# Filler matmuls at the start: the first ones on zeros, and a lower bar for the gaps that get them

## The chip, the cores and the metric

The kernel runs on one core of a Trainium2 chip. The metric is the device time of one execution in microseconds; of several runs the median is taken. Three runs of the kernel before took 624.91, 627.36 and 629.05 us, so the median is 627.36 us. The engines are named as in the profile: PE (TensorE matmuls, with PEld for its weight loads), DVE (VectorE), ACT (ScalarE), POOL (GpSimd) and SP (SyncE, which here only issues DMAs).

## What is computed

Block-causal attention over 8 batches, 8 heads, 576 positions and 64 columns per head, then a gated feed-forward network with a convolution over three positions:

```python
scores = scale * np.matmul(q, k.transpose(0, 1, 3, 2))      # 576 x 576 per head
scores = np.where(block_i >= block_j, scores, -1e9)          # blocks of 64
attn = exp(scores - max) / (sum + 1e-09)
x = (attn @ v)                                               # heads side by side: 576 x 512
h = np.maximum(x @ w_in, 0.0)                                # 512 -> 1024
conv_out = conv_w[0] * h[s - 1] + conv_w[1] * h[s] + conv_w[2] * h[s + 1]
out = (h * sigmoid(conv_out)) @ w_out                        # 1024 -> 512
```

## The kernel before, in words

Two heads are handled together as a pair; a batch has four pairs. For batch 0 each pair is done in two parts, first the first 256 positions (`stage_sa`, score products in line 1336, reductions to the row maximum in line 1354, exponentials in line 1362), then the rest (`stage_sb`, lines 1275 and 1291, with `last_s`, line 1123, for the last 64 positions). From batch 1 on a pair is done in one piece (`stage_s`, products in line 1111, maxima in line 1210, exponentials in line 1213). The probabilities are turned (line 1410, by matmuls with an identity) and multiplied with v (lines 1454 and 1494). The feed-forward network (`ffn`) multiplies with the two halves of w_in in line 1547 and with those of w_out in line 1640; the weights are decoded and split at the start by DVE, ACT and POOL (lines 885 to 963).

The order is written by a planner. Every operation is given to `Plan.op` with an engine, an estimated duration and a target; a long table of numbers replaces the targets. `Plan.order` then plays a clock of its own for five engines: `free[PE]` is the planned time at which PE is free, and it starts at zero (SP's at 0.75). It takes the operation that can start first and gives PSUM banks to tiles as it goes. The order in which operations come out is the order in which each engine's instructions are issued; semaphores hold the real order.

**Fills.** When the planner sees PE idle for longer than `LEAST` (0.4 us of planned time) and a PSUM bank is free, it puts matmuls there that compute nothing which is used: each multiplies the 128x128 identity (`rident`) with itself into 512 columns of the free bank (`work`, line 1777). Their number is the gap, less `SPARE` (0.09), divided by 0.234 us (twice that while the planner believes PE's clock to be low). In the kernel before there are 80 of them, in 17 places, the last of them 158 us into the span. A fill that has the tile `rident` as its operand cannot start before DVE has written that tile (line 645), which itself waits for POOL's `ident`. In `work` the operand would be the zeros in `blank` for any fill emitted before that write; since the write is emitted ahead of all fills, none uses it. `blank` is the first thing DVE writes (line 666).

The first products of the program are those of line 1336 for pair 0. They need q (loaded by SP's queue, scaled by POOL in line 1018) and k, whose DMA for this pair alone is issued by ACT's queue (line 701). Between pair 0 and pair 1 stands the small transpose of the convolution weights (line 1003).

Of the kernel before, what the change touches and what calls it, by code (L numbers as in the profile page):

```python
# [220 lines left out]
class Plan:  # L221
# [56 lines left out]
    def order(self, targets, fill, clock):  # L278
# [37 lines left out]
            for d in o.deps:  # L316
                d.outs.append(o)
        rtime, wtime, early = ([0.0] * len(self.ops) for _ in range(3))
        free = [0.0, 0.0, 0.0, 0.0, 0.75]
        port, begun, tail, moved = [0.0, 0.0, 0.0], -1.0, 0.2, 0.0  # L320
        done = []
        for _ in self.ops:
# [26 lines left out]
            if e == PE and t - free[PE] > least and t > begin:  # L349
                spot = [(max(free[PE], begun, freed[z]), z) for z in range(n) if tenant[z] is None]  # L350
                if spot:
# [3 lines left out]
                    if k > 0:  # L355
                        x = Op()
# [63 lines left out]
def kernel(  # L420
# [51 lines left out]
    JW = (JW0, JW1, JW2, JW3, JW4, JW5, JW6, JW7, JW8, JW9, JWA, JWB, JWC, JWD, JWE, JWF)  # L472
    JD = (JD0, JD1, JD2, JD3, JD4, JD5, JD6, JD7, JL8, JL9, JLA, JLB, JLC, JLD, JLE, JLF)
    EBLK = (2,3)
    LEAST, SPARE = 0.4, 0.09
    CLOCK = (3.413, 0.46, 0.33, 1.0, 0.098)
    GROUPS = {"A": ((0, 1),), "B": ((2,), (3,)), None: ((0, 1, 2), (3,))}
    NORMS = {"A": (), "B": (), None: ()}
# [159 lines left out]
    make_identity(nc, ident)  # L638
    rident = cp.tile([P, P], F32R, tag="rident", name="rident")

    rounded_one = []

    def rounded_identity():
        rounded_one.append(rident)
        nc.vector.tensor_scalar(out=rident, in0=ident, scalar1=1.0, scalar2=None, op0=ALU.mult)

    def constant(x, value):
# [3 lines left out]
        return go  # L651

    made = [pl.op(DVE, 0.2, rounded_identity, -80.0)]
    maskt = cp.tile([P, 64], F32R, tag="maskt", name="maskt")
    made.append(pl.op(ACT, 2.8, constant(maskt, MASKED), -80.0))
# [9 lines left out]
    blank = cp.tile([P, P], F32R, tag="blank", name="blank")  # L665
# [1102 lines left out]
    fills = []  # L1768

    def work(slot, k):  # L1770
        fills.append(k)

        def go():
            x = rident if rounded_one else blank
            b = psum[:, 512 * slot:512 * slot + 512]
            for _ in range(k):
                nc.tensor.matmul(b.rearrange("p (c n) -> p c n", n=P), x,
                                 x.unsqueeze(1).broadcast_to([P, 4, P]), start=True, stop=True)

        return go  # L1780

    ctx.enter_context(tc.manual_schedule(engines=None))
    for o in pl.order([int(x) for x in TARGETS.split()], (work, psum, 0.234, LEAST, SPARE), CLOCK):
        o.fn()
# [86 lines left out]
```

## Time and profile before

| | |
|---|---|
| profiled execution, device time | 626.53 us |
| its span, first to last instruction | 624.6 us |
| median of the three timed runs | 627.36 us (624.91 to 629.05) |
| mean granted TensorE clock | 0.995 |
| PE busy | 593.6 us, 95% |
| DVE busy | 536.5 us, 86% |
| ACT busy | 480.2 us, 77% |
| POOL busy | 388.8 us, 62% |

About 1.9 us of the profiled execution lie outside the span. Busy shares are means over stages with different limits. Where a row names who released an engine from its wait ("<-"), the name is the one whose signal came last. The ends of matmuls are modelled, so the ends of rows on PE are less exact than their starts.

### The profile page before, as it was taken

The numbers are of one execution on the slowest core, as the hardware profiler recorded it, in microseconds if no ns is written. First come the engines' busy times: TensorE is split into PE (matmuls) and PEld (weight loads), VectorE is DVE, ScalarE is ACT, GpSimd is POOL, SyncE is SP. The second block draws the span as 40 slices with busy tenths as digits, with TensorE's granted clock in tenths as the row PEclk, the third lists the DMA queues.
The fourth block names the chain that finished last, engine by engine and source line by source line (L and its number), as shares of the span: only waits on it lengthen the run. The fifth ranks groups of instructions, "written<-read, shape, count | busy, mean of one in ns | idle before, by whom it ended". The sixth has DMA issues, their size and how long they took to land.

```text
span 624.6 us, 15535 instructions
## 1 busy us (share of the span) xinstructions
PE 593.6 (95%) x5823; PEld 378.1 (61%) x5823; DVE 536.5 (86%) x1124; ACT 480.2 (77%) x1231; POOL 388.8 (62%) x498
## 2 busy tenths in 40 slices
PE   7888899977999999999999999999999999999997
PEld 4556554456765567655775577555765667566754
DVE  6999989999889988999999996999989957982741
ACT  5999998787688769997998687888787757963730
POOL 4876545584496656986687645765897615742630
PEclk9998989999999999999999999999999999999999
DMA  8783402799928996689966699179955970595002
GB/s 297 236 314 116 132 22 81 172 219 193 260 48 182 233 232 127 132 214 214 214 159 154 138 213 266 48 131 217 218 105 103 230 145 18 108 150 130 1 1 84
DMA packets 205503, 97.76 MB, mean 157 GB/s; under 512 B 185308, under 2 KB 187636, under 8 KB 205428
## 3 DMA queue, kind: packets, MB, share of 16 engines
q1 hardware_dynamic: 203844, 94.16, 68.1%
q10 hardware_dynamic: 1584, 2.62, 1.3%
q8 instruction: 45, 0.74, 0.5%
q14 instruction: 30, 0.25, 0.1%
HBM read 41.44 MB, written 9.44 MB: 81 GB/s over the span
## 4 chain that ended last, share of the span: by engine, by line
PE 37%; DVE 36%; ACT 10%; POOL 9%; issue 4%; DMA 3%; SPq 0%; ACTq 0%; DVEq 0%; POOLq 0%
PE banks L1640 14%; PE banks L1547 12%; DVE su L1210 7%; PE banks L1494 4%; PE banks L1111 4%; POOL t L1589 3%; DVE ptbl L1066 3%; DVE t L1576 2%; DVE ptbm L1066 2%; DVE t L1595 2%; POOL shared L1606 2%; DVE shared L900 1%; ACT t L1592 1%; DVE shared L895 1%; ACT p3f L1213 1%
## 5 line engine op out<-in xcount | busy, mean ns | idle before, releaser
L1640 PE MATMUL banks<-woh,shared 128*128 128x512 f16 (+1 forms) x592 | 184.0, 374 | 1.3 <-ACT p2f L1213 0.9
L1547 PE MATMUL banks<-x,wih 128*128 128x288 f16 (+2 forms) x1024 | 158.3, 288 | 5.1 <-ACT p4f L1213 1.6
L1640 PEld LDWEIGHTS <-shared 128*128 128x128 f16 x888 | 82.7, 98 | 101.3 <-issue 14.0
L1547 PEld LDWEIGHTS <-wih 128*128 128x128 f16 x1024 | 98.4, 98 | 40.5 <-issue 11.9
L1210 DVE TENSOR_REDUCE su<-banks 128x1 f32<-128x384 f32 (+8 forms) x252 | 110.2, 477 | 6.1 <-PE banks L1111 4.2
L1640 PE MATMUL banks<-wol,shared 128*128 128x512 f16 (+1 forms) x296 | 110.5, 373 | 0.0
L1589 POOL TENSOR_TENSOR t<-t,shared 128x575 f32<-128x575 f32 x51 | 73.4, 1440 | 49.4 <-DVE t L1576 44.9
L1547 PE MATMUL banks<-x,wil 128*128 128x288 f16 (+2 forms) x512 | 86.6, 287 | 0.0
L1111 PE MATMUL banks<-k,q 64*64 64x192 f32 (+9 forms) x1120 | 82.6, 417 | 3.3 <-ACT p1f L1213 1.3
L1606 POOL TENSOR_TENSOR shared<-t,shared 128x576 f16<-128x576 f32 (+2 forms) x57 | 71.3, 1253 | 16.8 <-ACT shared L1599 8.0
L1494 PEld LDWEIGHTS <-vb 128*64 128x64 f16 x1848 | 61.8, 111 | 12.6 <-issue 12.5
L1576 DVE SCALAR_TENSOR_TENSOR t<-banks,cwb,t 128x575 f32<-128x575 f32 (+2 forms) x72 | 53.4, 743 | 14.9 <-ACT t L1572 8.1
L1111 PEld LDWEIGHTS banks<-k,q 64*64 64x64 f32 x1120 | 43.0, 133 | 33.0 <-issue 14.1
L1592 ACT ACTIVATE t<-t 128x576 f32<-128x576 f32 (+2 forms) x72 | 45.1, 627 | 21.1 <-POOL t L1589 14.3
L1595 DVE SCALAR_TENSOR_TENSOR t<-t,banks 128x576 f32<-128x576 f32 (+2 forms) x72 | 48.9, 680 | 12.2 <-ACT t L1592 11.4
L1547 PEld LDWEIGHTS <-wil 128*128 128x128 f16 x512 | 49.5, 98 | 13.9 <-issue 0.6
L1572 ACT ACTIVATE t<-banks,cwb 128x576 f32<-128x576 f32 (+2 forms) x72 | 49.2, 685 | 2.0 <-POOL shared L1606 0.5
L1566 ACT ACTIVATE banks<-banks 128x576 f32<-128x576 f32 (+2 forms) x54 | 30.9, 577 | 18.6 <-PE banks L1547 16.7
L1585 ACT ACTIVATE shared<-banks,cwb 128x575 f32<-128x575 f32 x51 | 37.7, 738 | 8.6 <-DVE banks L1569 7.2
L1213 ACT ACTIVATE p3f<-banks,su 128x512 f32<-128x512 f32 (+1 forms) x56 | 36.8, 660 | 5.6 <-DVE su L1210 3.0
L1650 ACT ACTIVATE stage<-banks,osc 128x512 f32<-128x512 f32 (+1 forms) x27 | 18.0, 675 | 25.3 <-PE banks L1640 22.5
L1213 ACT ACTIVATE p1f<-banks,su 128x192 f32<-128x192 f32 (+1 forms) x56 | 24.9, 446 | 15.4 <-DVE su L1210 12.6
(204 smaller groups left out, 1190.4 us busy)
## 6 DMA issues: line engine op xcount, KB each, us to landing
k<-in_k_dram SPq DMA_DIRECT2D x28, 368.0 KB, 3.8
vn<-in_v_dram SPq DMA_DIRECT2D x32, 320.0 KB, 3.8
q<-in_q_dram SPq DMA_DIRECT2D x28, 320.0 KB, 3.6
out_dram<-stage SPq DMA_DIRECT2D x26, 256.0 KB, 3.0
shared<-in_moe_w_in_dram SPq DMA_DIRECT2D x8, 512.0 KB, 4.6
shared<-in_moe_w_out_dram SPq DMA_DIRECT2D x8, 512.0 KB, 4.7
out_dram<-stage ACTq DMA_DIRECT2D x9, 256.0 KB, 4.2
k<-in_k_dram SPq DMA_DIRECT2D x4, 240.0 KB, 5.6
```

The lines of the kernel that those rows point to most:

```text
L1111: nc.tensor.matmul(out[64 * y:64 * y + 64], t["q"].ap[64 * r:64 * r + 64, q0:q0 + 64], t["k"].ap[64 * r:64 * r + 64, k0:k0 + c1 - c0], sta ...
L1210: nc.vector.tensor_reduce(out=st.ap[:, k:k + 1], in_=home[hh].ap[:, x], op=ALU.max, axis=AX.X, negate=True)
L1213: nc.scalar.activation(out=y.ap[:, 0:n], in_=home[hh].ap[:, x], func=AF.Exp, bias=st.ap[:, k:k + 1], accum_out=st.ap[:, 9 + k:10 + k])
L1494: nc.tensor.matmul(y, vb.ap[:, w, c, j, :], x, start=first, stop=(z == 1 and c == jobs[-1][0]), skip_group_check=True)
L1547: nc.tensor.matmul(h(a, z), wt[:, c, fs], xs[c][xi].ap[:, x0 + a:x0 + z], start=(n + c - c0 == 0), stop=(n + c - c0 == 3 * NCC - 1))
L1572: nc.scalar.activation(out=t.ap[:, 0:no], in_=h(own, own + no), func=AF.Copy, scale=cwb.ap[:, NFC + f:NFC + f + 1])
L1576: nc.vector.scalar_tensor_tensor(out=t.ap[:, i0:no], in0=h(own + i0 - 1, own + no - 1), scalar=cwb.ap[:, f:f + 1], in1=t.ap[:, i0:no], op0 ...
L1589: nc.gpsimd.tensor_tensor(out=t.ap[:, 0:i1], in0=t.ap[:, 0:i1], in1=u.ap[:, 0:i1], op=ALU.add)
L1592: nc.scalar.activation(out=t.ap[:, 0:no], in_=t.ap[:, 0:no], func=AF.Tanh)
L1595: nc.vector.scalar_tensor_tensor(out=t.ap[:, 0:no], in0=t.ap[:, 0:no], scalar=1.0, in1=h(own, own + no), op0=ALU.add, op1=ALU.mult)
L1606: eng.tensor_tensor(out=g[1][:, f, carry:carry + no], in0=t.ap[:, 0:no], in1=g[0][:, f, carry:carry + no], op=ALU.subtract)
L1640: nc.tensor.matmul(fb.ap[:, 0:cut], g[a][:, f, cs], w[:, f, ds], start=(f == 0 and n == 0), stop=(f == NFC - 1 and n == 2))
```

## The change

Four edits. `free[PE]` starts at 1.1 instead of 0.0, so that the planner puts nothing on PE before 1.1 us of its own clock. `LEAST` falls from 0.4 to 0.25 and `SPARE` from 0.09 to 0.0, so that shorter planned gaps get fills and each gap may get one more. The first group of fills multiplies the zeros in `blank`, every other group `rident` as before (it is decided when the plan is made, by the count of groups so far). The list that was to tell whether `rident` had been written goes away, and with it two lines, so that every line behind it has a number lower by two.

```diff
-        free = [0.0, 0.0, 0.0, 0.0, 0.75]
+        free = [1.1, 0.0, 0.0, 0.0, 0.75]
...
-    LEAST, SPARE = 0.4, 0.09
+    LEAST, SPARE = 0.25, 0.0
...
-    rounded_one = []
 
     def rounded_identity():
-        rounded_one.append(rident)
         nc.vector.tensor_scalar(out=rident, in0=ident, scalar1=1.0, scalar2=None, op0=ALU.mult)
...
     def work(slot, k):
         fills.append(k)
+        x = rident if len(fills) > 1 else blank
 
         def go():
-            x = rident if rounded_one else blank
             b = psum[:, 512 * slot:512 * slot + 512]
```

On DVE, ACT, POOL and SP the instructions and their order are the same as before, and every tile keeps its PSUM bank. On PE only fills differ: 89 in 21 places instead of 80 in 17.

PE at the start of the program, before (`rident` is the identity, `cg` the convolution weights, `maskt` the mask that is added):

```order
L1777 MATMUL banks<-rident 128x512 x7
L1336 MATMUL banks<-k,q 128x128 x2
L1340 MATMUL banks<-maskt,rident 64x64 x2
L1336 MATMUL banks<-k,q 128x256 x2
L1340 MATMUL banks<-maskt,rident 64x64 x2
L1003 MATMUL banks<-ident,cg 128x24
L1777 MATMUL banks<-rident 128x512 x4
L1336 MATMUL banks<-k,q 128x128 x2
```

The same place with the change (`blank` is the tile of zeros):

```order
L1775 MATMUL banks<-blank 128x512 x5
L1334 MATMUL banks<-k,q 128x128 x2
L1338 MATMUL banks<-maskt,rident 64x64 x2
L1334 MATMUL banks<-k,q 128x256 x2
L1338 MATMUL banks<-maskt,rident 64x64 x2
L1775 MATMUL banks<-rident 128x512
L1001 MATMUL banks<-ident,cg 128x24
L1775 MATMUL banks<-rident 128x512 x5
L1334 MATMUL banks<-k,q 128x128 x2
```

Seven fills on the identity became five on zeros, and two more fills stand between the products of pair 0 and those of pair 1.

PE at the last turns of batch 0's third and fourth tile rows, ahead of the first products of a pair of batch 1, before (`p3r` are probabilities, `ptbh` turned ones):

```order
L1410 MATMUL banks<-rident,p4r_98 128x128 x4
L1410 MATMUL banks<-rident,p3r_94 128x128 x4
L1410 MATMUL banks<-rident,p3r_96 128x128 x4
L1777 MATMUL banks<-rident 128x512
L1111 MATMUL banks<-k,q 64x64 x2
L1111 MATMUL banks<-k,q 64x512 x2
```

The same place with the change:

```order
L1408 MATMUL banks<-rident,p4r_98 128x128 x4
L1408 MATMUL banks<-rident,p3r_94 128x128 x4
L1408 MATMUL banks<-rident,p3r_96 128x128 x4
L1775 MATMUL banks<-rident 128x512 x2
L1109 MATMUL banks<-k,q 64x64 x2
L1109 MATMUL banks<-k,q 64x512 x2
```

One fill became two. The other places that gain a fill: one ahead of pair 2's products of line 1336, one in a group of nine, one ahead of line 1454 (at 27.6 us before), one each in the groups at 34.9, 44.7, 70.1 and 143.4 us, and one ahead of the products of line 1111 at 100.7 us.

## Rows read from the trace of the kernel before

**Rows 1.** The page: busy time by engine; the chain that ended last, by engine.

```profile
PE 593.6 (95%) x5823; PEld 378.1 (61%) x5823; DVE 536.5 (86%) x1124; ACT 480.2 (77%) x1231; POOL 388.8 (62%) x498
...
PE 37%; DVE 36%; ACT 10%; POOL 9%; issue 4%; DMA 3%; SPq 0%; ACTq 0%; DVEq 0%; POOLq 0%
```

**Rows 2.** Chain that ended last, start: start us, us, what.

```profile
1.44 1.00 DVE rident L645
...
2.48 3.35 PE banks L1777 x7
5.83 0.73 PE banks L1336 x4
...
7.72 0.94 DVE st L1354 x3
```

**Rows 3.** Timeline of PE, 2 to 11 us: start, us, line, tiles [idle before].

```profile
2.48 3.35 PE L1777 MATMUL banks<-rident 128*128 128x512 f32 x7 [2.48 <-DVE rident L645]
5.76 0.80 PE L1336 MATMUL banks<-k,q 64*128 64x128 f32 x4
...
7.06 0.62 PE L1340 MATMUL banks<-maskt,rident 64*64 64x64 f32 x2
7.61 0.29 PE L1003 MATMUL banks<-ident,cg 24*128 24x24 f32 x1
7.84 1.20 PE L1777 MATMUL banks<-rident 128*128 128x512 f32 x4
8.96 0.49 PE L1336 MATMUL banks<-k,q 64*128 64x128 f32 x4
...
9.64 0.39 PE L1340 MATMUL banks<-maskt,rident 64*64 64x64 f32 x2
10.56 0.49 PE L1336 MATMUL banks<-k,q 64*128 64x128 f32 x4 [0.54 <-ACT q L1021]
```

**Rows 4.** Timeline of DVE and of ACT's DMA queue, same stretch.

```profile
0.83 0.17 DVE L666 MEMSET blank<- 128x128 f32 x1 [0.83 <-PEq L1854]
...
1.44 0.38 ACTq L701 DMA_DIRECT2D k<-in_k_dram  x1
...
7.71 0.95 DVE L1354 TENSOR_REDUCE st<-banks 128x1 f32<-128x256 f32 x3 [3.29 <-PE banks L1340]
...
10.59 2.23 DVE L1354 TENSOR_REDUCE st<-banks 128x1 f32<-128x128 f32 x8
```

**Rows 5.** DMA issues of the first 12 us: KB each, us to landing.

```profile
k<-in_k_dram ACTq DMA_DIRECT2D x1, 128.0 KB, 4.0
```

**Rows 6.** Stretches: busy us of each engine, granted clock (PEclk), DMA.

```profile
55.64:59.05 3.41, 1.49 (x14) 1.17 (x13) 3.41 (x8) 3.22 (x11) 3.33 (x4) 1.00 0.49 154
59.05:62.46 3.41, 3.41 (x20) 2.62 (x19) 3.41 (x8) 2.64 (x9) 2.95 (x4) 0.50 0.68 167
...
79.53:82.94 3.41, 3.41 (x21) 1.70 (x21) 2.78 (x4) 3.04 (x9) 3.33 (x5) 0.50 0.00 0
```

**Rows 7.** Timeline of PE around later places that gain a fill.

```profile
27.59 2.28 PE L1454 MATMUL banks<-ptbh,vn 128*64 128x320 f32 x20 [0.54 <-ACT ptbh L679]
...
34.87 1.67 PE L1777 MATMUL banks<-rident 128*128 128x512 f32 x6 [1.23 <-ACT p1f L1362]
36.68 0.88 PE L1410 MATMUL banks<-rident,p3r 128*128 128x128 f32 x8
...
71.78 1.13 PE L1275 MATMUL banks<-k,q 64*128 64x512 f32 x4 [0.29 <-DVE st L1134]
```

**Rows 8.** Chain that ended last, 45 to 105 us.

```profile
46.26 1.99 DVE wil L963 x3
...
79.48 1.21 PE banks L1410 x8
80.68 0.55 PE banks L1777
81.24 1.93 PE banks L1111 x8
...
83.26 0.83 DVE su L1210 x2
...
104.86 5.99 PE banks L1640 x27
```

## The prediction

> **What bounds the kernel now.** I read the page first. PE is busy for 593.6 of 624.6 us, but the chain that ended last is shared: 37% of it on PE and 36% on DVE [rows 1]. So the kernel has stages with different limits, and the change must be read where it acts: in the first 160 us, and there above all in the first 12, since fills stand nowhere later.
>
> Second, the chain of waits at the start. It runs from DVE's writing of the identity (1.44 us) through the seven fills (2.48 to 5.83) to the first score products of line 1336 and from 7.72 on through DVE, beginning with the maxima of line 1354 [rows 2]. Behind that it stays mostly on DVE up to the turns of 79.48 [rows 8]. The reader is to see that PE is late only once in the opening, at DVE's idle 3.29 us ahead of 7.71 [rows 4].
>
> Third, the timeline of PE there [rows 3]. The chain makes it look as if the fills held the products back. The DMA view says otherwise: k for pair 0 is issued by ACT's queue from 1.44 for 0.38 us [rows 4] and lands 4.0 us after that [rows 5], 1.44 + 0.38 + 4.0 = 5.82 within the rounding of the view. The products start at 5.76 [rows 3]. So the first product waits for k, and the seventh fill happened to end just then.
>
> Fourth, PE's clock. In the opening the duration of equal work tells it: seven fills take 3.35 us, 0.48 each, at 2.48 [rows 3]; six take 1.67, 0.28 each, at 34.87 [rows 7]. The products of pair 0 take from 5.76 to 7.06 + 0.62 = 7.68, 1.92 us; the same work for pair 1 from 8.96 to 9.64 + 0.39 = 10.03, 1.07 us [rows 3]. So PE ran at its lower level (1.2 GHz) up to about 7.7 and at 2.4 GHz soon after, having worked without a pause from 2.48. Twice more the granted clock is 0.50 for 3.41 us: at 59.05, after a stretch in which PE was busy for 1.49 of 3.41 us, and at 79.53 [rows 6].
>
> **The change part by part.**
>
> *Fills on zeros.* They need only `blank`, written at 0.83 to 1.00 [rows 4], not the identity. So PE can begin at about 1.05 instead of 2.48. Five fills at 0.48 end at about 3.5. The wait for the identity leaves the chain, but k still lands at 5.8, so the products start at 5.76 as now: the direct gain is 0. The mask products behind them now wait for the identity themselves; it is there by 2.44 [rows 2].
>
> *The clock at 5.76.* PE will have worked 2.4 us by 3.5 and then stand idle for 2.2 us. If the clock is up when k lands, pair 0's products take 1.07 us instead of 1.92: 0.85 us less, and since DVE waits for exactly them, it begins line 1354 at 6.86 instead of 7.71. If it is not, the gain is 0. The trace before shows neither case, so these are the bounds. I take 0.85: the fills' 2.4 us fall 1.4 us earlier, and all of pair 0's work lay in the slow stretch that the clock's rise ended at about 7.7, so any rise before 5.76 takes the whole of it.
>
> *Two more fills between pair 0 and pair 1* (one ahead of line 1003, one in the group of four). They delay pair 1's products by at most 2 x 0.28 = 0.56 us. Pair 1's products would end at 10.03 - 0.85 + 0.56 = 9.74; DVE, also 0.85 earlier, asks for them at 10.59 - 0.85 = 9.74 [rows 3, 4]. That is just covered: cost 0. If the first term fails, the cover is the 0.56 us between 10.03 and 10.59, again just enough at the higher clock. The fill ahead of pair 2 lies in the 0.54 us for which PE waits for ACT's q at 10.56 [rows 3]: 0.
>
> *Later fills.* The new one ahead of line 1454 lies in a wait of 0.54 us, and the sixth of 70.1 in front of one of 0.29 [rows 7]: 0 each. The seventh at 34.87 would end where the turns of 36.68 start anyway, 34.87 + 1.67 + 0.28 = 36.82 at most with the drain of the last counted in [rows 7], and DVE carries the chain there: 0. The fourth at 44.7 and the tenth at 17.9 stand where the chain is on DVE, as at 46.26 [rows 8]: 0; if that cover were gone, 0.28 each. The one ahead of line 1111 at 100.7 waits for DVE's earlier signal, and PE's work behind it waits again before it takes the chain at 104.86 [rows 8]: 0. The one at 143.4 likewise, 0 to 0.28.
>
> *The second fill at 80.7* is the exception. The chain goes through PE there: turns, one fill of 0.55, products, then DVE's maxima at 83.26 [rows 8]. The clock is at its lower level from 79.53 to 82.94 [rows 6], so one more fill costs about 0.48; at the higher level 0.28. I take +0.48.
>
> **Does the start reach the end?** 0.85 us earlier at 7.7 is worth something only if DVE stays the limit. DVE's share of the chain is as large as PE's [rows 1], and no DMA stands in the opening's rows of it [rows 2]. I let it pass whole; that it is lost on the way belongs to the second case below.
>
> **The sum**, against the profiled execution: 626.53 - 0.85 + 0.48 = 626.16 us. The median of the three runs, 627.36, lies 0.83 above that execution; the same step brings the forecast to **627.0 us**. In the last 65 us and in most of the middle no instruction changes.
>
> **The rivals.**
>
> A, the forecast: the clock is up by 5.76. Chance 0.40.
>
> B, nothing is gained at the start: the five fills on zeros do not raise the clock in time, or in most timed runs of the kernel before it was already up when k landed. For it: five fills are fewer than seven, and a pause of 2.2 us follows. Then only the fill at 80.7 counts: 627.36 + 0.48 = 627.8. Chance 0.29. The Trainium skill, page "TensorE: Matmul & The Clock Gate", Part 1 ("What's actually happening"), says that the moment of the rise is not tied to a kernel's start, so that the same kernel shows different numbers of slow matmuls from run to run. By that rule the gain is 0.85 in some executions and 0 in others, and the sum would be about 627.4, half way; one execution before cannot show it.
>
> C, slower: the pause keeps the clock down for longer. Before, PE's work was unbroken from 2.48 until the rise at about 7.7; now a pause of 2.2 us lies in it. If the clock is not up by 7.7, the next stretch is slow as well: a fill (0.48), line 1003 and five fills (2.4) bring PE from 7.7 to about 10.8, and pair 1's products, partly slow, end near 12.1 instead of 10.03, 2.05 late less the 0.56 that DVE has to spare, +1.5. With the fill at 80.7: 627.36 + 1.5 + 0.48 = 629.3. It decides if the products behind 7.7 are still slow. Against it: PE works without a pause from 5.76 on in that case too. Chance 0.19.
>
> D, the low clock at 79.53 goes away, because an earlier start or the sixth fill at 70 moves the quiet stretch ahead of it. Turns of eight take 0.88 at the higher clock [rows 7] and 1.21 there [rows 8]; with the fill and about half of the 1.93 of line 1111 some 1.5 us of the chain go, and the fill costs 0.28. On top of A: 627.36 - 0.85 - 1.5 + 0.28 = 625.3. Chance 0.12.
>
> That the change would not do what it says is small: the order shows the five fills on zeros first.
>
> **How the numbers follow.** The likeliest case gives 627.0. The cases lie between 625.3 and 629.3, and a median of runs that spread over 624.9 to 629.05 moves by about 1 us, so 8 in 10 needs **624.5 to 629.9**. A difference of 1% is 6.3 us, about what a measurement of this kernel can tell from no change; no row holds so much, all the fills added amount to 9 x 0.48 = 4.3 us even if none were covered. Faster by over 1%: 0.03; within 1%: 0.94; slower by over 1%: 0.03. These rests are for an effect of the shifted order that I do not see.
>
> **What would show it.** In the changed profile five fills on `blank` begin at about 1.05 and the first products still at 5.76. Right for A: pair 0's products take about 1.07 us and DVE's first maxima come at 6.9. B: they take 1.92 and DVE starts at 7.7. C: pair 1's products take well over 1.07 us and DVE waits ahead of its second maxima. D: no granted clock of 0.50 near 79. The chain should hold two fills of together about 1 us near 80. I am wrong if the products start well before 5.7, if one of the covered fills appears in the chain, or if the middle of the span, where nothing was changed, differs by more than the start does.

## The result, and the profile after

The changed kernel takes **629.94 us** (median of 5 runs, 629.31 to 631.30) where the kernel before took 626.54 (median of 5, 624.59 to 629.05): 1.0061 times as long, 95% interval 1.0042 to 1.0080. The forecast was 627.0 with a range up to 629.9. The median lies only 0.04 us beyond the range, and a second set of runs (f1 below) has 629.45, inside it; what is plainly wrong is the direction. The forecast step was -0.4 us (from 627.36, the median of three runs that was then known), the measured one is +3.4 here and +2.7 in f1. That is the side of rival C (629.3), which had a chance of 0.19. By the bound of 1% the result is still "within 1%".

The profiled execution after took 629.94 us, its span is 627.9 (before 626.53 and 624.6 [rows 1]). The page gives the busy time by engine, and the share of each engine in the chain of waits:

```profile
PE 596.1 (95%) x5832; PEld 380.8 (61%) x5832; DVE 536.5 (85%) x1124; ACT 480.6 (77%) x1231; POOL 388.5 (62%) x498
...
PE 43%; DVE 31%; POOL 9%; ACT 9%; DMA 5%; issue 3%; SPq 0%; ACTq 0%; DVEq 0%; POOLq 0%
```

PE's share of the chain rose from 37 to 43% at DVE's expense. The chain of waits from the start (start us, us, what) answers to [rows 2]:

```profile
1.45 4.67 DMA k<-in_k_dram
...
6.26 0.80 PE banks L1334 x4
...
8.17 0.72 PE banks L1775
8.89 0.23 PE banks L1001
9.12 2.43 PE banks L1775 x5
11.55 0.54 PE banks L1334 x4
```

The load of k stands at its head now, as the prediction said, and the identity is gone from it. But six fills (line 1775) have come into it behind pair 0's products; before, DVE had the chain from 7.72 on. The timeline of PE (start, us, line, tiles, idle before) answers to [rows 3]:

```profile
1.05 2.50 PE L1775 MATMUL banks<-blank 128*128 128x512 f32 x5 [1.05 <-DVE blank L664]
6.26 0.80 PE L1334 MATMUL banks<-k,q 64*128 64x128 f32 x4 [2.70 <-DMA k<-in_k_dram]
...
7.53 0.65 PE L1338 MATMUL banks<-maskt,rident 64*64 64x64 f32 x2
8.10 0.79 PE L1775 MATMUL banks<-rident 128*128 128x512 f32 x1
8.83 0.30 PE L1001 MATMUL banks<-ident,cg 24*128 24x24 f32 x1
9.05 2.50 PE L1775 MATMUL banks<-rident 128*128 128x512 f32 x5
11.49 0.61 PE L1334 MATMUL banks<-k,q 64*128 64x128 f32 x4
...
12.29 0.38 PE L1338 MATMUL banks<-maskt,rident 64*64 64x64 f32 x2
```

Read the fives: the five fills at 9.05 take 2.50 us, as long as the five at 1.05, which is 0.48 to 0.5 each and so the lower level (1.2 GHz). Before, the four at 7.84 took 1.20 [rows 3]. Pair 0's products and masks take 6.26 to 8.18, 1.92 us, just as before. Pair 1's last product ends at 12.29 + 0.38 = 12.67; before it was 10.03. In this trace the first recorded change of the granted clock, to full, is at 11.77 us; in that of before it is at 7.85. Up to here the one idle time of PE that is new is the pause of 2.70 us ahead of 6.26.

DVE's timeline shows who pays; it answers to [rows 4]:

```profile
8.18 0.95 DVE L1352 TENSOR_REDUCE st<-banks 128x1 f32<-128x256 f32 x3 [3.71 <-PE banks L1338]
...
12.71 1.15 DVE L1352 TENSOR_REDUCE st<-banks 128x1 f32<-128x128 f32 x4 [1.57 <-PE banks L1338]
```

The second maxima (those of pair 1) come at 12.71 instead of 10.59, 2.12 us late, behind a wait for PE that did not exist before. It stays: at DVE's first write of the tile `wil`, which started at 45.0 before, the changed kernel is at 47.4, 2.4 late (groups of one tile, first the kernel before and then the changed one; behind the durations stand the first start and the last start):

```profile
L963 DVE SCALAR_TENSOR_TENSOR wil<-shared,fac,wih x8: 731/738/884, 45.0 to 58.9; 128x512 f16<-128x512 f32 x8
L961 DVE SCALAR_TENSOR_TENSOR wil<-shared,fac,wih x8: 732/740/905, 47.4 to 61.4; 128x512 f16<-128x512 f32 x8
```

The DMA view answers to [rows 5]: k took 4.7 us to land where it took 4.0, so the products begin at 6.26 instead of 5.76.

```profile
k<-in_k_dram ACTq DMA_DIRECT2D x1, 128.0 KB, 4.7
```

That half microsecond is the execution's and not the change's: a second profile of the same kernel (f1 below) has the products at 5.78 and the second maxima at 12.97.

The stretches (us, busy us of PE, PEld, DVE, ACT and POOL, granted clock, DMA) answer to [rows 6]:

```profile
59.05:62.46 3.41, 2.16 (x21) 1.98 (x22) 3.41 (x7) 3.41 (x12) 3.24 (x4) 1.00 0.47 154
79.53:82.94 3.41, 3.00 (x26) 2.01 (x28) 3.29 (x8) 3.41 (x12) 3.03 (x4) 1.00 0.00 0
428.20:431.61 3.41, 1.36 (x15) 0.59 (x14) 3.38 (x11) 1.09 (x5) 1.38 (x2) 1.00 1.19 188
431.61:435.02 3.41, 3.07 (x50) 3.07 (x51) 0.87 (x3) 3.41 (x14) 0.31 (x1) 0.50 1.05 237
```

The two low stretches of before, at 59.05 and 79.53, are not in this execution; one at 431.61 is. Around 79.5 the chain answers to [rows 8]: PE is no longer in it, so the second fill there costs nothing.

```profile
80.89 0.39 DVE su L1208
81.28 0.70 DVE shared L898
...
84.13 0.82 DVE su L1208 x2
```

At 431 the chain goes through the output's write, from which the buffer `stage` comes free, and then through products at the low clock (1.2 GHz):

```profile
424.85 6.26 DMA out_dram<-stage
...
431.21 0.70 ACT stage L1648
431.95 3.75 PE banks L1492 x65
```

In the trace of before the same write took 5.24 us, and the products behind it start at 430.38 at the full clock (a line of its chain and one of its PE timeline):

```profile
424.30 5.24 DMA out_dram<-stage
...
430.38 1.07 PE L1494 MATMUL banks<-ptbx,vb 128*64 128x256 f16 x20 [1.34 <-ACT stage L1650]
```

DVE's lateness against that trace, instruction by instruction, is 2.33 us at 12.9, 2.56 at 59.7, 0.85 at 86 (where before had its own low stretch), 0.52 at 426.5 and 3.27 at 438 (moments of the trace of before). So two accounts were open: the start's 2.1 to 2.5 us last to the end and the profile of before only hides them by its own two low stretches; or they are regained in the middle, and the loss is the new stretch at 431.

### The profile page after: what moved, and what is told of

Same layout as the page of the kernel before. It is cut to its first block, busy times and chain, and to the rows that moved or that the text cites. A ratio compares the mean times of both kernels' runs of the same rounds, so it can differ in the third digit from the quotient of the medians.

```text
span 627.9 us, 15554 instructions
## 1 busy us (share of the span) xinstructions
PE 596.1 (95%) x5832; PEld 380.8 (61%) x5832; DVE 536.5 (85%) x1124; ACT 480.6 (77%) x1231; POOL 388.5 (62%) x498
## 4 chain that ended last, share of the span: by engine, by line
PE 43%; DVE 31%; POOL 9%; ACT 9%; DMA 5%; issue 3%; SPq 0%; ACTq 0%; DVEq 0%; POOLq 0%
PE banks L1638 17%; PE banks L1545 14%; DVE su L1208 6%; PE banks L1492 6%; PE banks L1109 5%; POOL t L1587 3%; DVE ptbl L1064 3%; POOL shared L1604 2%; DVE t L1574 2%; DVE ptbm L1064 2%; DVE t L1593 2%; DMA k<-in_k_dram 2%; ACT t L1590 1%; DVE vb L832 1%; DVE shared L898 1%
## 5 line engine op out<-in xcount | busy, mean ns | idle before, releaser
L1492 PEld LDWEIGHTS <-vb 128*64 128x64 f16 x1848 | 63.3, 113 | 13.6 <-issue 12.9
```

The source lines that it names most:

```text
L1492: nc.tensor.matmul(y, vb.ap[:, w, c, j, :], x, start=first, stop=(z == 1 and c == jobs[-1][0]), skip_group_check=True)
```

## The experiments

The kernels were run in three series (e, f, g). Each kernel has 12 runs against 35 runs of the kernel before in the same series. Ratios are to those, with 95% intervals. The medians of before in the three series were 627.18, 626.79 and 627.26. Fills compute nothing that is used, so every one of these kernels does the whole computation. Line numbers shift by one or two between them. The last two columns come from the one execution of each that was profiled: the moment at which the granted clock rose to full, and the start of DVE's second maxima.

| run | what it is | median us | ratio | clock rises, us | second maxima, us |
|---|---|---|---|---|---|
| f1 | the change, again | 629.45 | 1.0040 [1.0017, 1.0064] | 12.93 | 12.97 |
| e1 | the change, old bar of 0.4 | 629.41 | 1.0026 [1.0000, 1.0051] | 9.88 | 10.93 |
| e2 | before, new bar of 0.25 | 628.05 | 1.0017 [0.9998, 1.0036] | 6.36 | 10.07 |
| e3 | the change, 11 zeros for 5 | 626.80 | 0.9998 [0.9978, 1.0017] | 6.88 | 10.57 |
| e4 | the change, no fills between pairs 0 and 1 | 629.66 | 1.0031 [1.0014, 1.0048] | 15.79 | 11.02 |
| f2 | 11 zeros and the old bar | 627.15 | 0.9998 [0.9979, 1.0018] | 5.56 | 9.90 |
| f3 | the change, third `stage` buffer | 628.25 | 1.0012 [0.9990, 1.0035] | 13.75 | 13.44 |
| f4 | before, 5 fills for 7 | 626.90 | 1.0008 [0.9988, 1.0029] | 14.56 | 12.31 |
| g1 | before, third `stage` buffer | 626.06 | 0.9982 [0.9958, 1.0006] | 6.35 | 10.46 |
| g2 | f2 and the third `stage` buffer | 625.10 | 0.9971 [0.9948, 0.9995] | 4.92 | 9.85 |
| g3 | f2, 16 fills for 4 ahead of pair 1 | 628.14 | 1.0013 [0.9990, 1.0036] | 4.40 | 12.12 |
| g4 | before, 2 fills for 7 | 629.72 | 1.0041 [1.0015, 1.0066] | 14.40 | 12.12 |

The record also gives the mean granted clock of each execution. It does not see the opening, where the column reads 1.00 throughout; it falls by 0.5 x 3.41 / 625 = 0.0027 for one low stretch in the middle. So it tells roughly how many of those stretches an execution had. Of the 105 executions of the kernel before, 21 have 0.999 or more (mean 625.36 us), 60 have 0.996 to 0.998 (627.13) and 24 less (628.20).

**Which half of the change is it?** e1 keeps the start on zeros and puts the bar back; e2 does the reverse.

```
e1, against the change:
-    LEAST, SPARE = 0.25, 0.0
+    LEAST, SPARE = 0.4, 0.09
e2, against before:
-    LEAST, SPARE = 0.4, 0.09
+    LEAST, SPARE = 0.25, 0.0
```

> Only the start is changed: five fills on zeros from 1.05 us, planned from 1.1; LEAST and SPARE stay 0.4 and 0.09, so four fills stand between pair 0 and pair 1 and one fill ahead of 81 us. Theory P (the pause after the zeros keeps the clock low until about 11.8 us, and fills at the low clock then hold back pair 1's products): the clock rises near 11 to 12 us, DVE's second maxima start at about 12.0 (10.59 in the kernel before, 12.7 with the whole change; one fill and a half microsecond less than there), and the time is 1.5 to 3 us over the kernel before. Theory B (the lowered bar with its added fills costs the time): the second maxima start within 0.5 us of 10.6 to 11.1 and the time is that of the kernel before within 1 us.

> Only the bar is changed: LEAST 0.25 and SPARE 0.0; the first group is seven fills on the identity from 2.48 us as before. Theory P: the clock rises before 8.5 us as in the kernel before, DVE's second maxima start at 10.6 to 11.2, and the time is within 1 us of the kernel before. Theory B: DVE's second maxima start near 12 to 12.7 and the time is 2 to 4 us over the kernel before.

The start alone takes 0.26% more, the bar alone 0.17%; the first interval touches 1 and the second covers it. The runs point to the start but do not separate the two. The execution of e1 that was profiled was its fastest, 625.09 against a median of 629.41, and its clock rose at 9.88 already, so its page says little of the median.

**Is it the pause?** e3 leaves all of the change in and makes the first group 11 zeros, so that PE works right up to the arrival of k. If the pause is the cause, the loss goes; if it is that zeros do not count as work, or the eleven fills that the bar adds behind the first group (84 on the identity for 73 in e1), it stays.

```
-            for _ in range(k):
+            for _ in range(k if x is rident else 11):
```

> The whole change, but the first group is eleven fills on zeros instead of five, so that PE works without a pause from 1.05 us to about 5.9, when k lands. Theory P: the clock is up before the first products or at the latest where it was before (7.85), pair 0's products take 1.07 to 1.92 us, DVE's second maxima start at 9.8 to 10.7, and the time is 0 to 1 us under the kernel before. Theory Z (matmuls on zeros do not raise the clock, whatever their number): the clock rises at about 11.8 as with the whole change, the second maxima start at 12.7, and the time is 2 to 4 us over the kernel before.

The loss is gone, 0.9998. Its PE timeline:

```profile
1.05 5.06 PE L1775 MATMUL banks<-blank 128*128 128x512 f32 x11 [1.05 <-DVE blank L664]
6.24 0.78 PE L1334 MATMUL banks<-k,q 64*128 64x128 f32 x4
...
8.12 1.42 PE L1775 MATMUL banks<-rident 128*128 128x512 f32 x5
9.47 0.49 PE L1334 MATMUL banks<-k,q 64*128 64x128 f32 x4
```

The products start at 6.24, as late as in the profile after, yet the five fills at 8.12 take 1.42 us and not 2.50: the granted clock rose at 6.88. Pair 1 begins at 9.47, two microseconds before the changed kernel's. The bar's eleven fills are all still there, so they cost nothing that can be measured once the clock is up, and the clock rises behind zeros too. What e3 does not separate is the pause from the amount: it closes the pause by more than doubling the fills.

**Is it the six fills, which the prediction's rival C put in the way?** e4 takes only them out.

```
+        n = 0 if len(fills) in (2, 3) else k
...
-            for _ in range(k):
+            for _ in range(n):
```

> The whole change without the six fills between pair 0's and pair 1's products (one ahead of the small transpose, five behind it). If it is the fills at the low clock in front of pair 1's products that make DVE late, those products start at about 8.4 instead of 11.5, end at about 10.3 even at the low clock, and DVE's second maxima start at about 11.0 instead of 12.7: the time is 1 to 2 us under the whole change. If it is the low clock itself, whatever stands in the queue, the second maxima stay within 0.5 us of 12.7.

The time stays where it was (1.0031). PE's and DVE's timelines show why:

```profile
8.29 0.80 PE L1334 MATMUL banks<-k,q 64*128 64x128 f32 x4
...
10.99 0.80 PE L1334 MATMUL banks<-k,q 64*128 64x128 f32 x4
...
12.29 0.62 PE L1338 MATMUL banks<-maskt,rident 64*64 64x64 f32 x2
```

```profile
11.02 1.12 DVE L1352 TENSOR_REDUCE st<-banks 128x1 f32<-128x128 f32 x4
12.95 0.95 DVE L1352 TENSOR_REDUCE st<-banks 128x1 f32<-128x128 f32 x3 [0.81 <-PE banks L1338]
```

Four products take 0.80 us (0.49 at the full clock [rows 3]) at 8.29 and still at 10.99; here the clock rose only at 15.79. The second maxima are earlier, at 11.02, but the next wait for the slow products, and by 47.0 the first write of `wil` is as late as in the change. With the six fills the clock rose at 11.77 to 13.75 in three profiles (the change, f1, f3), without them at 15.79 in this one. So it may be that the fills both lengthen the bill of the low clock and help to end it, which one profile does not show; taking them out moved the bill and did not lower it by the 1 to 2 us that I expected.

**Does the change repeat, and is the new bar needed for the repair?** f1 is the change unaltered, f2 is e3 with the old bar.

```
f2, against the change:
-    LEAST, SPARE = 0.25, 0.0
+    LEAST, SPARE = 0.4, 0.09
...
-            for _ in range(k):
+            for _ in range(k if x is rident else 11):
```

> The whole change once more, unaltered. The earlier look showed one execution in which DVE was 2.3 us late at the start, 0.5 late at 421 us and 3.3 late at the end, with a stretch of low clock at 431.6. If the late end is that of the start alone (theory P), the second execution shows DVE 1 to 2.5 us late at 18 us, and the time over many runs is 1.5 to 3 us over the kernel before. If the stretch at 431 belongs to the change (theory S: the new timing puts that quiet stretch where the clock falls), a clock of 0.5 near 431 shows again and the time is 3 to 4 us over the kernel before.

> Eleven fills on zeros from 1.05 us, planned from 1.1, with LEAST 0.4 and SPARE 0.09 as before, so that no gap gets a longer fill. Theory P, with the nine added fills priced at what the bar alone showed (0 to 1 us): 0.5 to 1.5 us under the kernel before, since PE works without a pause and the clock rises by 7. If the pause were the only thing that counts and the clock of the opening is worth nothing beyond that: the time of the kernel before within 0.5 us.

f1 repeats the loss: 1.0040, products at 5.78, the same five fills in 2.50 us and the rise at 12.93. f2 gives 0.9998, and the gain of 0.5 to 1.5 us that I expected is not there although pair 0 does what case A of the prediction asked for:

```profile
1.05 4.87 PE L1775 MATMUL banks<-blank 128*128 128x512 f32 x11 [1.05 <-DVE blank L664]
...
7.10 1.19 PE L1775 MATMUL banks<-rident 128*128 128x512 f32 x4
```

```profile
7.02 0.95 DVE L1352 TENSOR_REDUCE st<-banks 128x1 f32<-128x256 f32 x3 [2.76 <-PE banks L1338]
...
9.90 2.23 DVE L1352 TENSOR_REDUCE st<-banks 128x1 f32<-128x128 f32 x8
```

The clock rose at 5.56, before the products (5.94), which with their masks take 1.07 us, and DVE starts 0.69 earlier than before. `wil` is written at 44.3 instead of 45.0, so the 0.7 us lives for 45 us at least; in the median of the whole it cannot be told from nothing (means of 626.99 and, for before, 626.73).

**Is it the pause in itself, with no zeros and no new bar?** f4 and g4 are the kernel before, with a first group of 5 or of 2 fills on the identity.

```
+        n = 5 if len(fills) == 1 else k        (g4: 2)
...
-            for _ in range(k):
+            for _ in range(n):
```

> The kernel before with five fills on the identity instead of seven in the first group, from 2.48 us to about 4.8, so that a pause of about 1 us stands ahead of the first products instead of 2.7 with the change and of none before. Theory P: the clock rises between 7.8 and 11.8 us depending on the moment, and the time is 0 to 1.5 us over the kernel before, between it and the start alone (1.6 over). If the number of fills decides and not the pause: as the start alone, 1.5 to 2.5 us over the kernel before.

> The kernel before with two fills on the identity instead of seven: PE works from 2.48 to about 3.5 and then pauses until k lands near 6, as with the change, but on the identity and not from 1.05. Theory P: as the start alone (629.4) or later, second maxima at 11 to 13, time 1.5 to 3 us over the kernel before. If the early start on zeros is what harms (theory Z) and not the pause: the time of the kernel before within 1 us, as with five fills on the identity (626.9).

g4 takes 1.0041 times as long, as the change does. PE's timeline has the same shape with none of the change in it:

```profile
2.49 1.22 PE L1778 MATMUL banks<-rident 128*128 128x512 f32 x2 [2.49 <-DVE rident L645]
6.09 0.80 PE L1336 MATMUL banks<-k,q 64*128 64x128 f32 x4 [2.38 <-DMA k<-in_k_dram]
...
8.16 2.07 PE L1778 MATMUL banks<-rident 128*128 128x512 f32 x4
10.17 0.80 PE L1336 MATMUL banks<-k,q 64*128 64x128 f32 x4
```

A pause of 2.38 us, and everything up to 10.17 and beyond runs at the low level; the clock rose at 14.40. f4 had a pause of 1.31 us in its profile:

```profile
2.48 2.50 PE L1778 MATMUL banks<-rident 128*128 128x512 f32 x5 [2.48 <-DVE rident L645]
6.29 0.80 PE L1336 MATMUL banks<-k,q 64*128 64x128 f32 x4 [1.31 <-DMA k<-in_k_dram]
...
10.36 0.80 PE L1336 MATMUL banks<-k,q 64*128 64x128 f32 x4
```

The clock rose at 14.56 there and `wil` is as late as 47.2, yet the median is 626.90, 1.0008. The granted clocks on record explain most of it: 6 of f4's 12 executions have 0.999 or more, against 8 of the 35 of before. Among those f4 takes 626.22 in the mean and before 624.82, and among the ones of 0.996 to 0.998 it takes 627.96 (4 executions) and before 626.80 (20). So at equal clock f4 is 1.2 to 1.4 us slower, and its neutral median is owed to fewer low stretches later on. The change (f1) is 2.7 slower in both groups (627.49, 3 executions, and 629.48, 6). f4 and the change have five fills each, so their number alone does not set the loss; the longer pause goes with the larger one. The groups are small, and f1 differs from f4 in the operand and the bar too. No run has five fills that end just as k lands, which would separate the pause from the amount of work ahead of the products; that rival stays open.

One thing speaks against the pause as the whole account. In the seven profiles with a pause of 1.31 us or more, PE worked all but without a break from pair 0's products on, and the clock still took 4.1 (e1) to 9.6 us (e4) of that to rise; in the seven with eleven zeros or seven identity fills it rose 3.4 to 5.8 us after the first fill. So unbroken work does not set the moment of the rise by itself; what else does, these runs do not tell.

**How much of a late pair 1 reaches the end when the clock is up?** g3 is f2 with 16 fills ahead of pair 1 in place of 4.

```
+        n = {1: 11, 2: 16}.get(len(fills), k)
...
-            for _ in range(k if x is rident else 11):
+            for _ in range(n):
```

> Eleven fills on zeros, so that the clock is up early, and sixteen fills instead of four between pair 0 and pair 1: these hold pair 1's products back by about 2.6 us at the higher clock. Theory P (lateness of DVE at its second maxima is what reaches the end, whatever made it): the second maxima start at 12 to 13 and the time is 1.5 to 3 us over the kernel with eleven zeros and four fills (627.15), so 628.5 to 630. If it is the low clock in itself that costs later on, or the change's other fills, the time stays within 0.7 us of 627.15.

```profile
7.16 3.94 PE L1776 MATMUL banks<-rident 128*128 128x512 f32 x16
11.03 0.49 PE L1334 MATMUL banks<-k,q 64*128 64x128 f32 x4
```

```profile
L961 DVE SCALAR_TENSOR_TENSOR wil<-shared,fac,wih x8: 736/741/889, 46.4 to 60.2; 128x512 f16<-128x512 f32 x8
```

The second maxima come at 12.12, 2.22 after f2's, and `wil` 2.1 after. The median is 1.0 over f2's, below the 1.5 to 3 that I expected, and its interval to before touches 1. g4, with its second maxima at 12.12 too but the clock low until 14.40, is at 47.1 for `wil` and 1.6 us slower than g3 in the median. So about one microsecond of the loss can come from plain lateness of pair 1. That the rest belongs to the slow work behind it is not shown: single medians here are good to about 1 us, and g4 also has more low stretches later on (6 of its 12 executions have a granted clock below 0.996, against 4 of g3's).

**Is it the stretch at 431?** Each kernel's output writes go through two buffers `stage`. With a third, the wait of 5 to 6 us on the write can go.

```
f3 against the change, g1 against before, g2 against f2:
-            ob = two([P, 512], F32, "stage")
+            ob = pl.buf(pt3, [P, 512], F32, "stage", 3)
```

> The whole change with three output buffers (stage) instead of two, so that the eviction at 431 us does not wait for an output DMA. Theory S: the quiet stretch and the low clock at 431 go away, and the time falls by about 2.8 us below the change, to that of the kernel before within 1 us. Theory P: that wait was in every kernel; it may take 0 to 1.5 us off here as it would off the kernel before, and DVE is still 1 to 2.5 us late at 18 us.

> The kernel before with three output buffers (stage) instead of two. With the change the third buffer took 1.2 us off (629.4 to 628.2). If that wait for an output DMA near 424 us is in every kernel, it takes 0.5 to 1.5 us off here too (625.4 to 626.4). If it was a part of what the change brought about (theory S), nothing changes here: the time of the kernel before within 0.4 us.

> Eleven fills on zeros, the old bar, three output buffers. If start and output buffer act on their own, 0.5 to 1.5 us under the kernel before; if the output buffer helps only late kernels, the time of the kernel before within 0.5 us. DVE's second maxima start at 9.9 to 10.7.

The third buffer takes 1.2 us off the change (f3 against f1), 1.2 off the kernel before (g1, with an interval that touches 1) and 2.0 off f2 (g2, in another series). It is worth about as much with the change as without it, so the wait at 424 is a loss of the kernel before, not the change's. A good part of the gain comes with a clock that stays up: with three buffers 18 of 36 executions have a granted clock of 0.999 or more, with two 5 of 24 (f1, f2) and 21 of the 105 of before. At equal clock f3 lies 0.5 to 0.8 us under f1, and g1 0.6 to 0.8 under before. And the difference between five zeros and eleven is there with three buffers as with two (f3 and g2, f1 and f2; they differ in the bar too, whose fills e3 has without a loss): 1.0012 - 0.9971 = 0.41%, against 1.0040 - 0.9998 = 0.42%, 2.6 us both times, each good to some 0.3%. So of the two accounts above the first holds: the loss is the start's, with no need of the wait at 424, and the stretch at 431 in the profile after is an execution's own, as those at 59 and 79 were in the profile of before. The same low stretch was in f1's profile (at 432.77) and in g3's (431.06), but in none of the other eleven profiles; how often each kernel falls into it was not measured. That f1 is 2.7 us slower than before at equal granted clock says the same.

**g2 is the one version whose interval lies below the kernel before**: 625.10 us, 0.9971 [0.9948, 0.9995]. Most of that lead is clock: 9 of its 12 executions have a granted clock of 0.999 or more, against 6 of the 35 of before, and among those it takes 624.93 in the mean and before 625.37. It was measured once, and it is the best of twelve.

## Why the prediction was wrong

By its own steps:

- *Fills on zeros.* Right: they begin at 1.05, five take 2.50 us, and the products wait for k all the same. The first product starts at 5.6 to 6.4 us in the profiles of these kernels.
- *The clock at 5.76.* **This is the step that failed.** It took -0.85 and gave the bounds as -0.85 and 0. The sentence "any rise before 5.76 takes the whole of it" was fine, as f2 shows (1.07 us for pair 0). The error lay in the bounds: the fills' work was moved, but it was also broken off, and the other end was not 0. With the pause the clock was still low when pair 0 was done: it rose at 11.77 and 12.93 in the two profiles of the change and at 9.88 to 15.79 in all seven with a pause of 1.31 us or more; with a pause of at most 0.62 it rose at 4.40 to 6.88 in those of 11 zeros and at 6.35 to 7.85 with seven fills on the identity. In place of a gain of 0.85 us, DVE's second maxima came 2.12 late. That the pause does it, and not the smaller amount of work ahead of the products, is the likelier reading and not proven (f4 above).
- *Two more fills between pair 0 and pair 1.* Their cover of 0.56 us was worked out at 0.28 each. At the low level the six, with line 1001 between them, held PE from 8.10 to 11.49, and the cover was long gone. The step hung wholly on the one above.
- *Later fills.* Right at 0: e3 keeps them and loses nothing. The bar adds eleven of them, not nine; nine is the difference after the first group lost two.
- *The second fill at 80.7.* +0.48 was wrong for the execution shown: there the clock was full and the chain went over DVE. It was priced on a low stretch that the profiled execution had and this one has not.
- *Does the start reach the end?* Too simple in both directions. f2's 0.7 us earlier does not show in the median, g3's 2.2 us later shows by about 1.0.
- *Rival C.* Its mechanism is what happened. It had pair 1's products end near 12.1; they end at 12.67 in the profile after, with k 0.50 later, and at 12.94 in f1's, with k as early as before. It priced the loss at 1.5 at the start and 0.48 at 80.7, in all 629.3; measured were 2.1 to 2.4 at the second maxima and nothing at 80.7, in all 629.45 and 629.94. That its total came so close is in part luck: it stands on a base of 627.36 where the medians of before were 626.54 and 626.79. Against it I set one sentence, that PE works without a pause from 5.76 on. It does, but that stretch began at 5.76 or later and not at 2.48, and the clock took another 5.5 (the profile after) and 7.2 us (f1) to rise. The trace of before showed no rise behind a pause, only one behind work that was unbroken. So the far end of the step's bounds was a clock that stays low through the fills and up to pair 1, and that end belonged into the step itself; put off into a rival, it got 0.19.
- *Rival D.* The low clock at 79.53 did go away in the profile after, without a gain in the median. Such a stretch is in some profiles and not in others: at 78.04 in e2's and 78.56 in e3's, and not in f1's.
- What I had named as a sign against myself, a covered fill in the chain, appeared: six of them.

The Trainium skill, page "TensorE: Matmul & The Clock Gate", Part 1, says that the moment of the rise is not tied to the kernel's start. The traces agree: the same change rose at 11.77 and at 12.93. In rival B I drew from it that the gain would be halved; the runs show that what PE did ahead of its first product mattered more than this scatter, with rises at 4.40 to 7.85 in seven profiles and at 9.88 to 15.79 in the other seven.

## What to carry to other kernels

Let warm-up work on PE reach up to the first real product: starting it earlier while letting it end earlier went with a loss of 0.3 to 0.6%, and the same earlier start with enough of it (11 zeros for 5) took the loss away. When an edit shortens a run of work ahead of a wait, price everything behind the wait at the low clock too, fillers first, since they cost more there (here 0.50 us each against 0.28) and may stand in front of the critical product. And before a low stretch or a long wait in one profile is charged to a change, put the same remedy on the kernel before: here it was worth as much there. Where each execution's granted clock is on record, compare executions of equal clock: that showed a loss in f4 that its median hid.

## What the runs showed of the hardware that I had not expected

- The granted clock rises behind work on zeros too: 11 fills on `blank`, with the rise at 6.88, 5.56, 4.92 and 4.40 us in four profiles; behind seven fills on the identity, which begin 1.43 us later, it rose at 7.85, 6.36 and 6.35.
- The column of the granted clock reads 1.00 ahead of the first change that the trace records, although the durations there (0.48 to 0.50 us for a fill, 0.80 for four products) show the low level. In an opening the clock is read from equal work.
- Low stretches, of 3.41 us (once 6.83, in e2), come in the middle of the span in some executions and not in others of one kernel, but only near four places in these fourteen profiles: 59 to 62 us, 78 to 80, 136 to 140 and 431 to 433. Ahead of each PE had been partly idle, as in the row of 428.20 above (1.36 of 3.41 us busy).
- They are a part of why runs of one kernel spread over some 5 us and more: the 105 executions of before go from 625.36 us in the mean at a granted clock of 0.999 or more to 628.20 below 0.996. They do not explain the change's loss, which is the same 2.7 us at equal clock.
